# Attention scores by head and tile on quarters of the matrix array, in steps of half a pair of heads

## The chip, the cores and the metric

One core of a Trainium2 chip. Its engines are PE (matrix products and transposes; PEld is its weight load), DVE and ACT (vector and activation work; they alone read PSUM), POOL (GpSimd, SBUF only) and SP, whose queue issues nearly all DMAs. Each engine works through its own queue in order and waits on semaphores. The metric is the device time of one execution in microseconds, lower is better; a time is the median of several runs.

## The reference, cut to what matters

Local attention with block summaries (4 batches, 8 heads, 768 positions, 64 per head), then a soft mixture of experts over the 3,072 tokens of 512 numbers, then a routed mixture. The part around the change:

```python
k_sum = k.reshape(B, H, nb, block, D).max(axis=3)      # 24 blocks of 32
v_sum = v.reshape(B, H, nb, block, D).mean(axis=3)
scores_l = scale * q @ k.T, kept where |i - j| < 16    # scale = 1/8
scores_s = scale * q @ k_sum.T + log(block)
a = softmax(concat([scores_l, scores_s], axis=-1))
out = a @ concat([v, v_sum])
logits = x @ phi                                       # x: out as (3072, 512); phi: 32 slots
```

All of it is float32.

## The kernel before

The 32 heads are worked off as 16 pairs (the two heads of a pair lie on partitions 0 to 63 and 64 to 127 of q and k). The 768 queries of a pair are 12 tiles of 64; a tile sees a window of 96 keys and the 24 block maxima, 120 columns (KW). For each pair:

- t_sum (L294) takes maxima over blocks of k on DVE, puts the 24 of them into k's tile with three small maxima (L308), and copies them into six places (L309), so that one slice of k holds window and maxima of a tile.
- q_prep (L285) copies q on DVE and on ACT or POOL into a block-diagonal tile of 128 x 128 for each query tile; its off-diagonal blocks are zeros, written once by the memsets of L228.
- s_pe (L311): one product per query tile for both heads, 128 x 128 stationary against 120 columns, four tiles to a PSUM bank. A float32 product is two PE instructions, so that four tiles are eight. Rows 0 to 63 of the result belong to one head, the others to the other.
- s_max (L322), DVE: adds the mask, multiplies by -1/8 and takes the row minimum, in one instruction per tile. s_exp (L341), ACT: one exponential per tile, with the row's extremum as its bias.
- p_pe (L347): four transposes into a PSUM bank; p_ev (L355) copies them out on ACT. v_pe (L360): 8 products (16 instructions) with v, whose 65th column of ones gives the denominator. v_norm (L378): three DVE instructions that divide into X.
- vs_pe, vs_dist, vs_out, vs_in (L253 to L283): block means of v. 24 PE instructions (on four strips of 32 columns), an ACT copy, a second product that brings the means to their rows, a second ACT copy, and two POOL copies (L280) into v's tile.
- x_pe, x_ev, x_log: X transposed, copied by ACT, multiplied by phi into the logits lp. At the end of a batch (four pairs) moe_a to moe_d keep a running softmax over tokens: moe_a (L428) extremum, exponential and a copy; moe_b (L456) four transposes; moe_b_ev eviction into L; moe_c (L476) twelve products with X into pa.

The work goes in steps u of a third of a pair (four tiles), 48 of them and a tail. The schedule is manual: each engine gets its instructions in the order in which the loop from L614 writes them. A step first does what earlier steps have prepared: copies of step u-3, maxima and exponentials of u-1, normalising of u-4; then PE's products: scores of u, transposes of u-2, values of u-3:

```python
if inr(u - 3): p_ev(u - 3)
if inr(u - 1): s_max(u - 1); s_exp(u - 1)
...
if inr(u): s_pe(u)
if inr(u - 2): p_pe(u - 2)
...
if inr(u - 3): v_pe(u - 3)
```

moe_a, moe_b and moe_b_ev of a batch come at u = 20 and 21 + 12b, moe_c at 21 + 12b. PSUM has eight banks: three for transposes, copies and sums (tag tr), two for s, two for po, one for lp. On SP, load_qk and load_v fetch the pair three ahead (1.65 MB a pair), and load_w fetches the 32 tiles of 1 MB of expert weights at the steps listed in W_STEPS; the tiles take buffers as v's tiles, X and the four fix tiles come free. At U_END the running softmax is closed; then the expert products (ph at L756, pO at L832, from w) and the routed part follow.

## Time and profile before

| what | us |
|---|---|
| median of 3 runs (290.44 to 291.0) | 290.75 |
| the profiled execution | 292.63 |
| its span, first to last instruction | 290.9 |
| busy PE / DVE / ACT / POOL | 264.1 / 176.7 / 158.1 / 53.6 |
| L317, the score products, x384 | 57.5 |
| L344, the exponentials, x192 | 60.4 |
| L329, mask and maxima, x192 | 42.6 |
| mean granted PE clock | 0.954 |

A profile is of one execution, so sums are made against its 292.63 us. Rows of the timeline give start, duration, engine, line, operation, written and read tiles, shapes and a count; consecutive instructions of one kind are merged. A matmul's duration runs until its last result, so the start of the next group shows how long PE's queue was held. The granted clock is a share of 2.4 GHz: 1.00 is 2.4 GHz, 0.50 is 1.2 GHz. "idle before" is the time that the engine sat idle ahead of the instruction, with what ended it.

### The profile page before, as it was taken

How to read it: one execution, taken by the hardware profiler on the slowest of the kernel's cores; microseconds unless marked ns; L12 is line 12 of the kernel's file. 1: busy time of each engine (PE TensorE's matmuls, PEld its weight loads, DVE VectorE, ACT ScalarE, POOL GpSimd, SP SyncE). 2: the span in 40 equal slices, each digit the busy share in tenths (PEclk: the TensorE clock that was granted, in tenths of full speed). 3: DMA queues.
4: the chain of work that ended last, by engine and by line, in shares of the span. 5: the costliest groups of instructions: out<-in, count | busy, mean ns of one | idle time of the engine just before them, and what ended most of it. 6: DMA issues, size and time to landing. Idle time of an engine off the chain costs nothing.

```text
span 290.9 us, 7301 instructions
## 1 busy us (share of the span) xinstructions
PE 264.1 (91%) x2686; PEld 185.9 (64%) x2686; DVE 176.7 (61%) x798; ACT 158.1 (54%) x411; POOL 53.6 (18%) x78
## 2 busy tenths in 40 slices
PE   5899999997999979999969999999899999769990
PEld 1689888886688856888856844323256683546770
DVE  4499888985788885797854633116112547555950
ACT  2588876784568755568755731122323647923550
POOL 2122212230442123142302001000010361010000
PEclk9999999997999997999998999999999959996997
DMA  6999989899198997356455899999959100011893
GB/s 216 404 391 385 368 308 324 293 335 325 53 359 259 288 351 262 90 183 231 146 189 165 266 392 400 394 386 387 333 172 379 37 0 0 0 30 43 321 392 119
DMA packets 33657, 72.55 MB, mean 249 GB/s; under 512 B 2713, under 2 KB 4377, under 8 KB 33617
## 3 DMA queue, kind: packets, MB, share of 16 engines
q1 hardware_dynamic: 33552, 71.83, 69.3%
q8 instruction: 23, 0.38, 0.5%
q0 software_dynamic: 64, 0.20, 0.3%
q14 instruction: 18, 0.14, 0.1%
HBM read 65.73 MB, written 6.29 MB: 248 GB/s over the span
## 4 chain that ended last, share of the span: by engine, by line
PE 75%; DVE 14%; ACT 3%; issue 2%; DMA 2%; SPq 1%; DVEq 0%; ACTq 0%
PE s L317 15%; PE po L369 8%; PE pt L352 6%; PE pO L832 5%; PE ph L756 5%; PE pv L262 4%; PE pht L1049 4%; PE tx L402 3%; PE lp L420 3%; PE pa L491 3%; DMA vw<-in_vw_dram 2%; PE py L1292 2%; DVE fix L329 2%; PE py L1293 2%; PE py L1294 2%
## 5 line engine op out<-in xcount | busy, mean ns | idle before, releaser
L317 PE MATMUL s<-fix,fix 128*128 128x120 f32 x384 | 57.5, 295 | 0.3 <-DVE fix L291 0.3
L317 PEld LDWEIGHTS s<-fix,fix 128*128 128x128 f32 x384 | 48.6, 198 | 8.7 <-issue 6.3
L280 POOL COPY vw<-vw 24x780 f32<-24x780 f32 x32 | 26.8, 837 | 103.6 <-ACT vw L270 100.5
L344 ACT ACTIVATE fix<-fix,nb 128x120 f32<-128x120 f32 x128 | 40.3, 394 | 9.4 <-DVE nb L329 9.4
L329 DVE CUSTOM_DVE_ANT_0 fix<-s,con 128x120 f32<-128x120 f32 x128 | 28.5, 277 | 21.4 <-PE s L317 15.2
L369 PEld LDWEIGHTS po<-vw,pts 120*64 120x64 f32 x768 | 26.8, 139 | 11.1 <-issue 5.4
L369 PE MATMUL po<-vw,pts 120*64 120x65 f32 x768 | 33.5, 230 | 0.0
L357 ACT COPY pts<-pt 120x512 f32<-120x512 f32 x48 | 28.4, 593 | 7.9 <-PE pt L352 7.6
L270 ACT COPY vw<-pv 128x130 f32<-128x130 f32 x32 | 8.6, 270 | 30.7 <-PE pv L262 27.8
L386 DVE TENSOR_TENSOR X<-po,den 128x256 f32<-128x256 f32 x48 | 20.4, 424 | 1.7
L262 PE MATMUL pv<-vw,con 120*32 120x130 f32 x384 | 14.8, 278 | 6.9 <-DVE L L470 5.1
L352 PE MATMUL pt<-con,fix 128*120 128x128 f32 x128 | 20.7, 288 | 0.0
L344 ACT ACTIVATE sm<-sm,nb 128x120 f32<-128x120 f32 x64 | 20.1, 393 | 0.0
L1062 DVE CUSTOM_DVE_ANT_0 hlo<-pht,scr 128x1024 fp32r<-128x1024 f32 x11 | 13.3, 1213 | 10.0 <-PE pht L1049 10.0
L1049 PE MATMUL pht<-cT,gs 128*128 128x512 f32 x48 | 16.7, 476 | 0.6 <-ACT hhi L1073 0.4
L1073 ACT ACTIVATE hhi<-pht,scr 128x1024 fp32r<-128x1024 f32 x13 | 14.5, 1115 | 3.9 <-PE pht L1049 3.7
L832 PE MATMUL pO<-w,hx 128*32 128x512 f32 (+1 forms) x160 | 16.2, 514 | 0.0
L412 ACT COPY xT<-tx 128x512 f32<-128x512 f32 (+1 forms) x32 | 14.9, 464 | 2.1 <-PE tx L402 2.1
L402 PE MATMUL tx<-con,X 128*128 128x128 f32 x96 | 15.9, 274 | 0.0
L329 DVE DVE_READ_ACCUMULATOR2_ANT nb<- 128x1 f32 x192 | 15.8, 82 | 0.0
L262 PEld LDWEIGHTS pv<-vw,con 120*32 120x32 f32 x384 | 9.9, 109 | 9.1 <-DVE L L470 5.7
L352 PEld LDWEIGHTS pt<-con,fix 128*120 128x120 f32 x128 | 15.5, 147 | 0.1
(242 smaller groups left out, 426.2 us busy)
## 6 DMA issues: line engine op xcount, KB each, us to landing
w<-in_moe_w_dram SPq DMA_DIRECT2D x30, 1024.0 KB, 8.4
vw<-in_vw_dram SPq DMA_DIRECT2D x32, 390.0 KB, 8.6
fix<-in_kT_dram SPq DMA_DIRECT2D x15, 484.0 KB, 4.8
out_dram<-Y SPq DMA_DIRECT2D x24, 256.0 KB, 2.6
qn<-in_qT_dram SPq DMA_DIRECT2D x8, 384.0 KB, 5.1
fix<-in_qT_dram SPq DMA_DIRECT2D x7, 384.0 KB, 5.0
w1e<-in_moe_w_dram SPq DMA_DIRECT2D x4, 512.0 KB, 5.6
w2e<-in_moe_w_dram SPq DMA_DIRECT2D x4, 512.0 KB, 9.3
```

The lines of the kernel that those rows point to most:

```text
L262: nc.tensor.matmul(pv[32 * g : 32 * g + 32, 0:130], con[:KW, b0 : b0 + 32], vw[:KW, par, x0 : x0 + 130], start=c == 0, stop=c == 2,)
L280: nc.gpsimd.tensor_copy(st_["vw", n][row0 : row0 + NB, par].rearrange("p (s x) -> p s x", s=6), vo[row0 : row0 + NB, 130:260].unsqueeze(1) ...
L317: nc.tensor.matmul(sp[:, i, :], qbds[n % NQB][:, t, :], kTs[n % NKT][:, o : o + KW], start=True, stop=True)
L329: nc.vector.tensor_tensor_reduce(out=sm[:, i, :], in0=sp[:, i, :], in1=con[:, m0 : m0 + KW], scale=-0.125, scalar=3.0e38, op0=ALU.add, op1 ...
L344: nc.scalar.activation(sm[:, i, :], sm[:, i, :], AF.Exp, bias=nb_[:, i : i + 1], scale=-1.0)
L352: nc.tensor.transpose(pv[:, i, :], pr[:, i, :], ident)
L357: nc.scalar.copy(pts, st_.pop(("pt", u)))
L369: nc.tensor.matmul(po[64 * i : 64 * i + 64, c, j, :], pts[:, 2 * c + i, j * 64 : j * 64 + 64], vw[:KW, i, (t // 2) * 130 + 65 * j : (t // ...
L386: nc.vector.tensor_tensor(out=X[:, 2 * g : 2 * g + 2, 2 * hp * D : (2 * hp + 2) * D].rearrange("p c (j d) -> p c j d", j=2), in0=po[:, :, ...
L402: nc.tensor.transpose(pt[:, c * P : c * P + P], st_["X", b][:, c0 + c, hp * P : hp * P + P], ident)
L832: nc.tensor.matmul(po[c][32 * g : 32 * g + 32, 0 : cs.stop - cs.start], hTs[r][:, fc, 32 * g : 32 * g + 32], w[:, g, cs], start=(r, fc) in ...
L1049: nc.tensor.matmul(ph[:, c * 512 : c * 512 + 512], G[:, k * P : (k + 1) * P], cTt(1024 * j + 512 * c, 512), start=True, stop=True,)
```

## The change

Steps become halves of a pair (NU = 32, six query tiles each). s_pe makes a product for each head and tile, 64 x 64 stationary: its rows of the array are those of the head j, its columns those of the tile's parity i, so the four products of a pair of tiles lie on four quarters; head j has its own PSUM bank, and rows 0 to 63 of a result are an even tile, 64 to 127 an odd one. q is read as it was loaded; q_prep and the memsets go, and q gets three buffers. The masks shrink to three. s_exp subtracts the extremum on GpSimd, three tiles at once, and takes one exponential of 360 columns on ACT. t_sum writes the 24 maxima once and then takes the maxima of both halves straight into all six places. p_pe and its copy, v_pe and v_norm work on three tiles of two heads. The loop is written anew: scores, maxima and exponentials of u, then values and normalising of u-2, then the V-block sums, transposes of X, logits and batch ends, then transposes and copies of u-1. moe_a, moe_b and moe_c come at u = 13, 14 and 16 + 8b. s has three banks, po one. The weights are asked for at other steps. The order of the block means (C_DIST) is changed to fit.

The diff, cut to its core; removed lines of functions and of the loop are those of the kernel above and are mostly left out, as are shapes of PSUM tiles, masks and index constants:

```diff
-VS_FIRST = (0, 2)
-
 C_STEPS = (6, 7, 8, 9, 10, 11, 12, 13)
-W_X, W_BIG2, W_BIG3 = 14, (13, 15, 16, 17), (20, 21)
-U_END = 20 + 12 * (B - 1)
-W_STEPS = (*range(6, 36, 3), 39, 41, 43, 45, 46, 48, 49, 50, 51, 52)
+W_X, W_BIG2, W_BIG3 = 17, (13, 14, 16, 18), (20, 21)
+U_END = 13 + 8 * (B - 1)
+W_STEPS = (*range(4, 26, 2), 27, 29, 30, 30, 31, 32, 32, 33, 33)
...
-        ps_s = es.enter_context(tc.tile_pool(name="ps_s", bufs=2, space=PSUM))
-        ps_o = es.enter_context(tc.tile_pool(name="ps_o", bufs=2, space=PSUM))
+        ps_s = es.enter_context(tc.tile_pool(name="ps_s", bufs=3, space=PSUM))
+        ps_o = es.enter_context(tc.tile_pool(name="ps_o", bufs=1, space=PSUM))
...
+        NU = 2 * NPAIR
+        kTs = [fix[2][:, 0:KTW], fix[0][:, 0:KTW], fix[0][:, KTW : 2 * KTW]]
+        qns = [fix[2][:, KTW : KTW + S], fix[1][:, 0:S], fix[1][:, S : 2 * S]]
+        sms = [fix[3][:, i * 6 * KW : (i + 1) * 6 * KW].rearrange("p (j c x) -> p j c x", j=2, c=3) for i in range(2)]
+                nc.sync.dma_start(out=qns[0][:, 0:384], in_=qT[0, :, 0:384])
+            nc.sync.dma_start(out=kTs[n % 3], in_=kTd[n])
+            nc.sync.dma_start(out=qns[n % 3], in_=qT[n])
...
-        def q_prep(n):
...
+            hb = hm[:, 0:48].rearrange("p (b r) -> p r b", r=2)
+            nc.vector.tensor_tensor(out=kT[:, 32 : 32 + NB], in0=hb[:, 0], in1=hb[:, 1], op=ALU.max)
+            nc.vector.tensor_tensor(
+                out=kT[:, 32 + NB :].rearrange("p (c x) -> p c x", x=152)[:, :, 128:152],
+                in0=hb[:, 0:1].to_broadcast([P, 6, NB]),
+                in1=hb[:, 1:2].to_broadcast([P, 6, NB]),
+                op=ALU.max,
+            )
+
+        def s_pe(u):
+            n, h = divmod(u, 2)
+            sp = [ps_s.tile([P, 512], F32, tag="s", name=f"s{u}_{j}")[:, 0 : 3 * KW] for j in range(2)]
+            sp = [x.rearrange("p (c x) -> p c x", c=3) for x in sp]
             for c in range(3):
+                for i in range(2):
+                    t = 6 * h + 2 * c + i
+                    o = _koff(t)
+                    for j in range(2):
+                        nc.tensor.matmul(
+                            sp[j][64 * i : 64 * i + 64, c, :],
+                            qns[n % 3][64 * j : 64 * j + 64, 64 * t : 64 * t + 64],
+                            kTs[n % 3][64 * j : 64 * j + 64, o : o + KW],
+                            start=True, stop=True,
+                        )
             st_["s", u] = sp
 
+        def s_max(u, j):
+            sp = st_["s", u][j]
+            if j == 0:
+                st_["nb", u] = p3.tile([P, 2, 3], F32, tag="nb", name=f"nb{u}")
+            for c in range(3):
+                e = 3 * (u % 2) + c
+                m0 = C_MASK + (0 if e == 0 else 2 if e == 5 else 1) * KW
                 nc.vector.tensor_tensor_reduce(
+                    out=sms[u % 2][:, j, c, :],
+                    in0=sp[:, c, :],
                     in1=con[:, m0 : m0 + KW],
                     scale=-0.125,
                     scalar=3.0e38,
                     op0=ALU.add,
                     op1=ALU.min,
+                    accum_out=st_["nb", u][:, j, c : c + 1],
+                )
+
+        def s_exp(u, j):
+            sm = sms[u % 2][:, j]
+            nc.gpsimd.tensor_tensor(
+                out=sm, in0=sm, in1=st_["nb", u][:, j].unsqueeze(2).to_broadcast([P, 3, KW]), op=ALU.subtract
+            )
+            nc.scalar.activation(sm, sm, AF.Exp, scale=-1.0)
 
         def p_pe(u):
+            pts = p2.tile([KW, 2, 3, P], F32, tag="pts", name=f"pts{u}")
+            for j in range(2):
+                pt = ps_tr.tile([P, 512], F32, tag="tr", name=f"pt{u}_{j}")[:KW, 0 : 3 * P]
+                pt = pt.rearrange("p (c x) -> p c x", c=3)
+                for c in range(3):
+                    nc.tensor.transpose(pt[:, c, :], sms[u % 2][:, j, c, :], ident)
+                nc.scalar.copy(pts[:, j], pt)
             st_["pts", u] = pts
 
         def v_pe(u):
+            n, h = divmod(u, 2)
             pts = st_.pop(("pts", u))
             vw = st_["vw", n]
+            po = ps_o.tile([P, 3, 2, 65], F32, tag="po", name=f"po{u}")
+            for c in range(3):
                 for j in range(2):
                     for i in range(2):
+                        x0 = (3 * h + c) * 130 + 65 * j
                         nc.tensor.matmul(
                             po[64 * i : 64 * i + 64, c, j, :],
+                            pts[:, j, c, 64 * i : 64 * i + 64],
+                            vw[:KW, i, x0 : x0 + 65],
                             start=True,
                             stop=True,
                         )
             st_["po", u] = po
...
+            den = p3.tile([P, 3, 2], F32, tag="den", name=f"den{u}")
+                out=X[:, 3 * h : 3 * h + 3, 2 * hp * D : (2 * hp + 2) * D].rearrange(
+                in1=den.unsqueeze(3).to_broadcast([P, 3, 2, 64]),
+        XP = ((0, 3), (3, 3))
...
+        last = B - 1
+
+        def vs(n):
+            vs_pe(n)
+            vs_out(n, 0)
+
+        def vs2(n):
+            vs_dist(n)
+            vs_out(n, 1)
+            vs_in(n)
+
+        for u in range(NU + 11):
             inr = lambda w: 0 <= w < NU
+            m, odd = divmod(u, 2)
             if inr(u):
                 s_pe(u)
+                for j in range(2):
+                    s_max(u, j)
+                    s_exp(u, j)
             if inr(u - 2):
+                if (u - 2) % 8 == 0:
+                    st_["X", (u - 2) // 8] = xp.tile([P, 6, DM], F32, tag="X", name=f"X{(u - 2) // 8}")
+                v_pe(u - 2)
+                v_norm(u - 2)
+            if u == 1:
+                p_pe(0)
+                vs(0)
+                vs2(0)
+                vs(1)
+                vs2(1)
+            vn = m + 1 if odd and 0 < m < NPAIR - 1 else None
+            if vn is not None:
+                vs(vn)
+            if (n := at(u, 3, 2, NPAIR)) is not None:
+                x_pe(n, 0)
+                x_ev(n, 0)
+            if (n := at(u, 4, 2, NPAIR)) is not None:
+                x_pe(n, 1)
+                x_ev(n, 1)
+            if (n := at(u, 6, 2, NPAIR)) is not None:
                 x_log(n)
+            if (b := at(u, 13, 8, B)) is not None:
+                moe_a(b)
+            if (b := at(u, 14, 8, B - 1)) is not None:
+                moe_b(b)
+                moe_b_ev(b)
+            if (b := at(u, 16, 8, B - 1)) is not None:
+                moe_c(b)
+                moe_c_ev(b)
+            for i in range(3):
+                if (b := at(u, 16 + i, 8, B)) is not None:
+                    moe_d(b, i)
+            if vn is not None:
+                vs2(vn)
+            if inr(u - 1) and u > 1:
+                p_pe(u - 1)
+            if odd and m + 1 < NPAIR:
+                t_sum(m + 1)
             if u == U_END:
                 keep_warm(2)
                 si_max()
@@ -661,7 +660,7 @@
                 moe_b(last)
                 moe_c(last, 0)
                 keep_warm(1)
+                moe_b_ev(last)
                 si_bc()
                 si_bc_ev()
                 moe_c(last, 1)
@@ -672,25 +671,16 @@
                 keep_warm(1)
                 siT_done()
                 keep_warm(1)
             if u == 0:
                 load_qk(2)
                 load_v(2)
+            if odd and m < NPAIR - 3:
+                load_qk(m + 3)
+                load_v(m + 3)
             if u == 3:
                 nc.sync.dma_start(out=con[:, C_SEL:], in_=consts[:, C_SEL:])
                 nc.sync.dma_start(out=phis, in_=phi.rearrange("(c p) s -> p c s", p=P))
+            for _ in range(W_STEPS.count(u)):
                 load_w()
     big3.append(ctx.enter_context(tc.tile_pool(name="big3", bufs=len(W_BIG3))))
```

## Rows read from the trace of the kernel before

**Rows 1.** Windows: stretch, span, busy PE, PEld, DVE, ACT, POOL; clock, DMA, GB/s
```profile
39.52:48.17 8.65, 8.65 (x125) 7.37 (x122) 7.16 (x42) 6.21 (x19) 2.86 (x3) 1.00 0.92 322
...
56.83:68.24 11.41, 9.51 (x130) 7.78 (x126) 9.12 (x48) 6.78 (x21) 2.85 (x3) 1.00 0.91 318
68.24:80.33 12.09, 12.09 (x135) 9.25 (x135) 7.82 (x39) 6.52 (x20) 3.35 (x4) 0.86 0.48 160
```

**Rows 2.** Timeline of PE: start, duration, instruction, count, idle before
```profile
68.24 0.88 PE L262 MATMUL pv<-vw,con 120*32 120x130 f32 x24 [1.63 <-DVE L L470]
...
72.99 1.92 PE L491 MATMUL pa<-X,L 128*32 128x512 f32 x12
...
80.33 0.88 PE L262 MATMUL pv<-vw,con 120*32 120x130 f32 x24
81.13 1.15 PE L317 MATMUL s<-fix,fix 128*128 128x120 f32 x8
82.12 0.61 PE L352 MATMUL pt<-con,fix 128*120 128x128 f32 x4
82.56 0.39 PE L273 MATMUL pv<-vw,con 128*128 128x130 f32 x2
82.88 0.69 PE L369 MATMUL po<-vw,pts 120*64 120x65 f32 x16
83.50 1.15 PE L317 MATMUL s<-fix,fix 128*128 128x120 f32 x8
...
85.46 0.63 PE L420 MATMUL lp<-xT,phis 128*32 128x256 f32 x6
```

**Rows 3.** Lines by form, POOL: count, busy us, mean ns, idle before
```profile
L518 POOL TENSOR_TENSOR ce_all<-L,mx 128x192 f32<-128x192 f32 x4 | 2.0, 507 | 17.3 <-DVE mx L517 17.3
...
L928 POOL TENSOR_TENSOR Y<-Y 128x384 f32<-128x384 f32 x1 | 1.0, 1002 | 0.1
...
L1119 POOL TENSOR_TENSOR scr<-scr 128x256 f32<-128x256 f32 x1 | 0.6, 616 | 2.3 <-ACT scr L1118 2.3
```

**Rows 4.** Lines by form, ACT
```profile
L522 ACT ACTIVATE ce_all<-ce_all 128x192 f32<-128x192 f32 x4 | 1.5, 365 | 2.0 <-POOL ce_all L518 2.0
...
L933 ACT ACTIVATE scr<-scr 128x24 f32<-128x24 f32 x1 | 0.2, 211 | 0.0
```

**Rows 5.** Timeline of all engines, at the start and about 158
```profile
7.79 1.21 PE L317 MATMUL s<-fix,fix 128*128 128x120 f32 x8
...
9.04 0.28 DVE L329 CUSTOM_DVE_ANT_0 fix<-s,con 128x120 f32<-128x120 f32 x1 [0.23 <-PE s L317]
...
9.86 0.08 DVE L329 DVE_READ_ACCUMULATOR2_ANT nb<- 128x1 f32 x1
...
157.89 0.34 DVE L517 TENSOR_REDUCE mx<-L 128x6 f32<-128x192 f32 x1
...
158.38 0.51 POOL L518 TENSOR_TENSOR ce_all<-L,mx 128x192 f32<-128x192 f32 x1 [1.63 <-DVE mx L517]
```

**Rows 6.** Timeline of all engines, in mid-batch
```profile
42.84 1.74 POOL L280 COPY vw<-vw 24x780 f32<-24x780 f32 x2 [6.92 <-ACT vw L270]
...
43.50 0.37 DVE L308 TENSOR_TENSOR fix<-hm 128x8 f32<-128x8 f32 x3
...
43.90 0.78 DVE L309 COPY fix<-fix 128x144 f32<-128x144 f32 x1
```

**Rows 7.** Timeline of PE at three places, and one window of DMA
```profile
15.78 1.12 PE L317 MATMUL s<-fix,fix 128*128 128x120 f32 x8 [0.25 <-DVE fix L291]
...
151.31 2.06 PE L317 MATMUL s<-fix,fix 128*128 128x120 f32 x8
...
168.48 1.15 PE L420 MATMUL lp<-xT,phis 128*32 128x256 f32 x6
...
216.77 1.07 PE L832 MATMUL pO<-w,hx 128*32 128x256 f32 x16
...
210.00:215.00 5.00, 4.59 (x65) 2.58 (x69) 0.93 (x6) 2.02 (x4) 1.01 (x6) 1.00 0.23 63
```

More of the change, by code (lines that the diff above doesn't have):

```diff
@@ L78, in _constants @@
         m[:, ssl] = 8.0 * LOGB
-        c[:64, C_MASK + var * KW : C_MASK + (var + 1) * KW] = m
-        c[64:, C_MASK + var * KW : C_MASK + (var + 1) * KW] = m
+        for e in range(3):
+            if var == (2 if e == 0 else 0) or var == (3 if e == 2 else 1):
+                r0 = 64 * (var % 2)
+                c[r0 : r0 + 64, C_MASK + e * KW : C_MASK + (e + 1) * KW] = m
     for g in range(4):
@@ L279, in vs_in @@
             for row0, par in ((32, 0), (96, 1)):
-                nc.gpsimd.tensor_copy(
+                eng = nc.vector if n == 0 and par else nc.gpsimd
+                eng.tensor_copy(
                     st_["vw", n][row0 : row0 + NB, par].rearrange("p (s x) -> p s x", s=6),
@@ L304, in t_sum @@
             )
-            hb = hm[:, 0:48].rearrange("p (h c q b r) -> p r c b q h", h=2, c=3, q=2, b=2)
-            ks = kT[:, 32:56].rearrange("p (q h c b) -> p c b q h", q=2, h=2, c=3)
-            for c in range(3):
-                nc.vector.tensor_tensor(out=ks[:, c], in0=hb[:, 0, c], in1=hb[:, 1, c], op=ALU.max)
-            nc.vector.tensor_copy(kTv[:, :, 128:152], kT[:, 32:56].unsqueeze(1).to_broadcast([P, 6, 24]))
-        def s_pe(u):
-            n, g = divmod(u, 3)
-            sp = ps_s.tile([P, 4, KW], F32, tag="s", name=f"s{u}")
-            for i in range(4):
-                t = 4 * g + i
-                o = _koff(t)
-                nc.tensor.matmul(
-                    sp[:, i, :], qbds[n % NQB][:, t, :], kTs[n % NKT][:, o : o + KW], start=True, stop=True
-                )
-            st_["s", u] = sp
@@ L322, in s_max @@
-        def s_max(u):
-            g = u % 3
-            sp = st_.pop(("s", u))
-            sm = sms[u % 3].rearrange("p (i x) -> p i x", i=4)
-            nb_ = p3.tile([P, 4], F32, tag="nb", name=f"nb{u}")
-            for i in range(4):
-                m0 = C_MASK + _var(4 * g + i) * KW
+            hb = hm[:, 0:48].rearrange("p (b r) -> p r b", r=2)
[6 more added lines that the diff above has]
+            )
@@ L611, in tile_kernel @@
         t_sum(0)
-        q_prep(0)
-        for u in range(NU + 32):
-            inr = lambda w: 0 <= w < NU
-            if inr(u - 3):
-                p_ev(u - 3)
-            if inr(u - 1):
-                s_max(u - 1)
-                s_exp(u - 1)
-            if (n := at(u, 1, 3, NPAIR - 1)) is not None and n or u == 2:
-                t_sum(n + 1 if n else 1)
-                q_prep(n + 1 if n else 1)
-            if inr(u - 4):
-                if (u - 4) % 12 == 0:
-                    st_["X", (u - 4) // 12] = xp.tile([P, 6, DM], F32, tag="X", name=f"X{(u - 4) // 12}")
-                v_norm(u - 4)
-            for i in range(2):
-                if (n := at(u, 8 + i, 3, NPAIR)) is not None:
-                    x_ev(n, i)
-            for r, f in enumerate((moe_a, moe_b_ev, moe_c_ev)):
-                if (bb := at(u, 20 + r, 12, B)) is not None and (r < 2 or bb < B - 1):
-                    f(bb)
-            for i in range(3):
-                if (bb := at(u, 22 + i, 12, B)) is not None:
-                    moe_d(bb, i)
+        last = B - 1
@@ L639, in tile_kernel @@
+        def vs(n):
[6 more added lines that the diff above has]
+        for u in range(NU + 11):
+            inr = lambda w: 0 <= w < NU
+            m, odd = divmod(u, 2)
             if inr(u):
                 s_pe(u)
+                for j in range(2):
+                    s_max(u, j)
+                    s_exp(u, j)
             if inr(u - 2):
-                p_pe(u - 2)
-            for n in range(NPAIR):
-                if u == (VS_FIRST[n] if n < 2 else 3 * n - 1) + 1:
-                    vs_dist(n)
-                    vs_out(n, 1)
-                    vs_in(n)
@@ L648, in tile_kernel @@
-            for i in range(2):
-                if (n := at(u, 7 + i, 3, NPAIR)) is not None:
-                    x_pe(n, i)
-            if (n := at(u, 10, 3, NPAIR)) is not None:
-                x_log(n)
-            if inr(u - 3):
-                v_pe(u - 3)
-            last = B - 1
+                if (u - 2) % 8 == 0:
[8 more added lines that the diff above has]
+                vs2(1)
@@ L674, in tile_kernel @@
                 keep_warm(1)
-            for r, f in enumerate((moe_b, moe_c)):
-                if (bb := at(u, 20 + r, 12, B)) is not None and bb < last:
-                    f(bb)
-            for n in range(NPAIR):
-                if u == (VS_FIRST[n] if n < 2 else 3 * n - 1):
-                    vs_pe(n)
-                    vs_out(n, 0)
             if u == 0:
@@ L684, in tile_kernel @@
                 load_v(2)
-            if (n := at(u, 2, 3, NPAIR - 3)) is not None:
-                load_qk(n + 3)
-            if (n := at(u, 1, 3, NPAIR - 3)) is not None:
-                load_v(n + 3)
+            if odd and m < NPAIR - 3:
+                load_qk(m + 3)
+                load_v(m + 3)
             if u == 3:
```

73 lines of the change are left out of this document (10 added, 63 removed).

## The prediction

> **What bounds the kernel now.** I read the windows pair by pair first. A pair of heads in mid-batch takes 8.65 us and PE is busy for all of it; DVE has 1.5 us to spare, ACT 2.4, and the DMA rings run at 0.92 [rows 1]. So until the logits are done the end is set by PE, and its timeline gives the prices: eight score instructions hold the queue 0.99 us (81.13 to 82.12), four transposes 0.44, the second V-block product 0.32, sixteen value instructions 0.62, the 24 V-block sums 0.80, six logit instructions about 0.56 [rows 2]. Three score groups make 3 us of the 8.65.
>
> The second reading is the batch ends. The two pairs around the first take 11.41 and 12.09 us [rows 1], 6.2 more than two plain ones; two more batch ends look alike. Only 2.3 of it is work (pa 1.9, four transposes 0.44). In the first of these pairs PE is idle for 1.9 us, its longest wait being 1.63 us on DVE's eviction of L; in the next its granted clock averages 0.86, that is, part of it ran at 1.2 GHz [rows 1, 2]. This loss comes from moe_a, moe_b and the eviction following one another within one step.
>
> After the logits (168.48 and about 1.1 us more [rows 7]) come some 121 us of expert work that the diff leaves alone.
>
> **The change, part by part.** I call one u of the new loop a step: two to a pair, odd ones carry the V-block work.
>
> *Scores.* 384 instructions on the whole array become 768 on quarters, 24 a step. What a quarter costs isn't in the trace. Nearest are the V-block sums: four strips at once, 130 columns, 0.80/24 = 33 ns each [rows 2]. Floor: a pa instruction of 512 columns on three strips costs 1.92/12 = 160 ns, scaled to 120 columns and four tiles 28. Ceiling: today's 0.99/8 = 124 ns with only two of four tiles at once, 62. I take 35, near the sums: 0.84 us a step, 1.7 a pair where 3.0 stand now. All else on PE keeps its count (48 value instructions, 12 transposes to a pair), so PE's work falls to about 7.4 us a pair. Were PE still the bound, that would be 1.3 us times 16.
>
> *But the loop is no longer staggered.* Before, step u evicted, maximised and exponentiated what earlier steps had left. After it, ACT's queue holds, in this order: exp(u,0), exp(u,1), the V-block copy, x_ev, the second V-block copy, the copies of p_pe(u-1). Both exponentials need this step's own scores, by way of DVE and GpSimd, and everything behind them waits too. From the start of an odd step:
> - scores 0.84; DVE starts 0.2 after the last issue (group at 7.79, DVE at 9.04, 1.25 where the queue is held 1.0) [rows 5]
> - first three maxima: four took 9.04 to 9.94, so three 0.70 [rows 5]
> - hand-over to GpSimd 0.15 (158.23 to 158.38) [rows 5]
> - two subtractions of 360 columns. Broadcast rows give 507 ns at 192 and 616 at 256, so 790 at 360; two full operands took 1002 at 384, about 950 at 360, my upper bound [rows 3]. 2 x 0.79 = 1.58; DVE's second trio lies beside it.
> - ACT: 211 ns at 24 columns, 365 at 192, so 520 at 360 [rows 4]; its start after GpSimd I estimate at 0.05, at most the 0.15 above.
>
> That is 4.05 us. Then the V-block copy (about 0.2 behind the exponential), vs_dist on PE 0.32, six transposes 0.66: the next step starts at 5.25. PE's own work in an odd step is only 4.0, so it idles 1.25. The even step has nothing on PE that waits for its own exponential: scores 0.84, values 0.92, three transposes 0.42, logits 0.56, six transposes 0.7, together 3.45. A pair is 8.7 against 8.65: **the time won on the array goes into the wait.** What is late next is the value products of the odd step (their copies come 1.75 after its start); they end with the V-block sums and transposes at 3.9, before 4.3, and cost nothing. Bounds: scores at 28 ns take 0.2 off each step; subtractions at 0.95 add 0.3 to the odd one.
>
> *Off the path.* ACT gets 4 exponentials of 0.52 a pair for 12 short ones; q_prep goes from DVE, ACT and GpSimd; normalising is done in two calls. All had slack, cost nothing and gain nothing. GpSimd takes 4 x 0.79 beside two copies of 0.87 [rows 6]: 4.9 of 8.7. The s banks (three, two to a step) are freed by DVE within the step; the one value bank is freed a step before its next use.
>
> *Block maxima.* Two tensor_tensor with two SBUF inputs replace three small ones and a copy. They come 5.0 us into the odd step, when GpSimd starts its two V copies, and the next maxima need DVE at 6.25. Rows: while L280 ran from 42.84 to 44.58, three L308 took 0.37 and were not held, but the copy L309 took 0.78 and ended as GpSimd did [rows 6]. I charge nothing here, at most one copy's 0.65, which fits before 6.25. The Trainium skill, SBUF — State Buffer, "Who interferes with whom", says a DVE instruction with two SBUF inputs is fully blocked for the whole GpSimd instruction. L308 disagrees, L309 agrees. By that rule the sum would be the rival of the port below.
>
> *Batch ends.* moe_a, moe_b and moe_c now lie in steps 13, 14 and 16, each with a step between to be evicted in. I leave the 2.3 of work and 0.75 for moe_a's DVE and ACT work ahead of the V-block copy: 3.05 where 6.2 stands now, -3.15 three times, **-9.5**.
>
> *Start.* Step 1 holds both first V-block sums, with t_sum(1) behind a DVE copy that waits for them. By the prices above p_pe(0) ends near 13, the two V chains near 16.7, t_sum(1) near 18.3, when pair 1's scores start; now 15.78 [rows 7]. **+2.5.**
>
> *End.* Now 168.48 plus 1.1 less 151.31 [rows 7] is 18.3 from the last pair's first scores, 14.9 without the batch end's 3.4. After: 3.45 for step 30, then one after the other: exponential 4.05, copies 1.2, values 0.9, transposes and logits 1.0, pa 1.9, transposes 0.7, copies 0.8, values 0.9, normalising 1.0, last transposes, copy and logits 1.6 (durations as above, copies and normalising estimated at 0.45 and 0.95 each): 17.5 in all, less pa 15.6. **+0.7.**
>
> *DMA.* A pair still moves 1.65 MB and about one weight tile, 2.7 MB in 8.7 us, as now. On SP load_qk, load_v and load_w keep their order; each pair waits for the release of its k buffer. Weights 13 to 19 are asked for in steps 30 to 33, as early against the logits as now. The rings are idle from 210 to 215 (0.23 busy) while pO's last tiles run on to 217.8 (216.77 and 1.07) [rows 7], which covers the few us by which consumption moves up. Nothing.
>
> Sum: 14 pairs x 0.05 = +0.7, +2.5, +0.7, -9.5 = **-5.6 us**. The profiled execution took 292.6 (span 290.9); the sum gives it 287.0, and the median of 290.75 becomes **285.2**.
>
> **Rivals.**
> - *PE or a shorter chain decides* (faster still): if ACT's copy can start by 3.5 rather than 4.05 and scores cost 28 ns, a pair is 7.8, -0.9 x 14 beyond the sum, 273. For: every hand-over is one row only. Against: the chain has 4 us of durations from rows. 15%.
> - *The port* (slower): both tensor_tensor wait for both V copies, DVE is free at 7.0, the next maxima come 0.8 late, so do the copies for the values, and from an extra 0.35 on the odd step stretches with them: +0.5 x 14 = +7, 292. It decides if L309's behaviour is the rule and L308's the exception [rows 6]. 18%.
> - *The clock.* Every odd step idles 1.25 us. At the batch end 1.9 us of idle in 11.4 was followed by a stretch at 1.2 GHz worth 1.5 us (12.09 less 8.65 less pa) [rows 1, 2]. If this comes in every pair, +1.0 to 1.5 x 14, 299 to 306. Against: the gaps are in pieces of at most 0.9. 13%. The Trainium skill, TensorE: Matmul & The Clock Gate, Part 1, second failure mode, warns of frequent small idles that make the clock oscillate; rows 1 and 2 show a fall only after the long one.
> - *Quarters don't run side by side* (the change doesn't do what it says): 62 ns an instruction, +0.65 a step, +1.3 x 15 = +19, 304. Against: strips do run side by side. 8%.
> - The forecast itself: 46%.
>
> **How the numbers follow.** The forecast's own range is 279 to 290 (subtractions at the bound +4, scores at the floor -5). The whole range must leave out no more than 2 in 10: the far half of the first rival and the upper parts of the clock and the quarters go, so 274 to 300. Below 0.2% (0.6 us) a measurement of this kernel can't tell a difference from none. Faster: the first case, nearly all of the forecast and a little of the port, 0.61; same 0.05; slower 0.34 from the port, the clock and the quarters.
>
> **What would show it.** Right: pair windows of 8.7 with PE idle about 1.2; the V-block copy on ACT starting 4 to 4.3 us after the odd step's first score, its wait put down to the exponential and that to GpSimd; 24 score instructions in 0.8; no pair over 11 us and no clock of 0.86 at batch ends. Wrong: score groups over 1.2 us; tensor_tensor of t_sum at 0.8 or more; granted clock under 0.95 over the attention; pair windows under 8.0, which would mean that ACT does not queue as the loop is written.

## The result and the profile after

The changed kernel takes **293.48 us** (median of five, 292.42 to 294.52) against 290.75 for the kernel before (five beside it, 288.82 to 291.0): a ratio of 1.0104, 95% interval 1.0061 to 1.0147. A later set on another occasion gave 293.17 against 289.44, ratio 1.0122 (1.005 to 1.0194). It is slower by about 1%, where 2% faster was forecast. In all runs below the medians are of all executions, while the ratios leave out those over 1.5% above the fastest of their version. The profiled execution of after took 292.89 us with a span of 291.1; that of before took 292.63 and was 1.9 above the median of its kernel, so the two profiles differ by less than the medians do.

Where the time went is read from the first scores of pairs. The timeline of PE, before (start, duration, instruction, count):

```profile
23.19 1.15 PE L317 MATMUL s<-fix,fix 128*128 128x120 f32 x8
...
57.64 1.15 PE L317 MATMUL s<-fix,fix 128*128 128x120 f32 x8
...
89.79 1.15 PE L317 MATMUL s<-fix,fix 128*128 128x120 f32 x8
...
139.59 0.59 PE L317 MATMUL s<-fix,fix 128*128 128x120 f32 x3
```

and after, with idle time ahead of an instruction and what ended it in brackets:

```profile
26.70 0.85 PE L302 MATMUL s<-fix,fix 64*64 64x120 f32 x24
...
60.89 0.85 PE L302 MATMUL s<-fix 64*64 64x120 f32 x24
61.66 0.92 PE L354 MATMUL po<-vw,pts 120*64 120x65 f32 x24
...
64.36 0.85 PE L302 MATMUL s<-fix 64*64 64x120 f32 x24
65.61 1.18 PE L354 MATMUL po<-vw,pts 120*64 120x65 f32 x24 [0.41 <-ACT pts L342]
...
68.42 0.49 PE L260 MATMUL pv<-vw,con 128*128 128x130 f32 x2 [0.35 <-ACT vw L257]
68.75 0.82 PE L341 MATMUL pt<-con,fix 128*120 128x128 f32 x6
71.29 1.05 PE L302 MATMUL s<-fix,fix 64*64 64x120 f32 x24 [1.72 <-DVE fix L285]
...
75.81 0.54 PE L341 MATMUL pt<-con,fix 128*120 128x128 f32 x3 [0.77 <-ACT xT L397]
...
91.75 0.85 PE L302 MATMUL s<-fix 64*64 64x120 f32 x24
...
140.01 0.84 PE L302 MATMUL s<-fix,fix 64*64 64x120 f32 x24
...
150.60 1.68 PE L302 MATMUL s<-fix 64*64 64x120 f32 x24 [1.90 <-DVE fix L285]
...
160.93 1.69 PE L354 MATMUL po<-vw,pts 120*64 120x65 f32 x24 [1.87 <-ACT pts L342]
...
171.29 1.13 PE L584 MATMUL warm<-con 128*128 128x256 f32 x4
...
179.86 0.64 PE L746 MATMUL ph<-w,siT 128*32 128x512 f32 x4
```

After less before, pair by pair: pair 2 starts 3.5 us later (26.70 against 23.19), pair 6 3.3 (60.89, 57.64), pair 9, behind the first batch end, 2.0 (91.75, 89.79), pair 14, behind the second, 0.4 (140.01, 139.59). Pair 15 starts 0.7 earlier (150.60; before in [rows 7]). Then it is lost again: the logits are done at 171.29 where the warm-up products behind them stood at 169.56, and the first product of the experts is at 179.86 instead of 178.21, 1.65 later. So the start cost 3.5, the plain pairs behind it gave 0.3, two batch ends with the plain pairs around them gave 1.3 and 1.5, the third with its pair 1.1, and the last pair cost 2.4.

The windows of after show a step each: an even and an odd step in mid-batch, the pair they make, then steps 13, 14 and 16 of the first batch end (step 15 is a plain odd one of 5.13), and five stretches for the clock. Columns are the stretch, its length, busy us (instructions) of PE, PEld, DVE, ACT and POOL, granted clock, DMA share and GB/s.

```profile
43.67:47.14 3.47, 3.47 (x65) 2.49 (x64) 2.13 (x15) 1.25 (x4) 3.04 (x4) 1.00 0.89 323
47.14:52.28 5.14, 4.34 (x85) 3.29 (x84) 3.56 (x19) 3.57 (x10) 1.70 (x3) 1.00 1.01 341
43.67:52.28 8.61, 7.81 (x148) 5.79 (x147) 5.69 (x34) 4.82 (x13) 4.74 (x7) 1.00 0.96 334
...
64.36:71.29 6.93, 4.41 (x85) 3.30 (x84) 4.56 (x21) 4.57 (x13) 3.20 (x4) 1.00 0.93 307
71.29:76.29 5.00, 4.23 (x68) 2.98 (x68) 2.85 (x17) 1.76 (x4) 1.53 (x2) 1.00 0.65 248
...
81.42:86.61 5.19, 5.19 (x77) 2.99 (x76) 2.81 (x17) 2.24 (x6) 3.04 (x4) 1.00 0.87 321
...
10.00:20.00 10.00, 6.67 (x109) 4.64 (x102) 4.78 (x26) 3.74 (x10) 5.23 (x7) 0.88 1.03 403
...
110.00:120.00 10.00, 7.20 (x142) 5.29 (x143) 6.73 (x36) 3.45 (x9) 3.91 (x5) 1.00 0.65 230
...
150.00:160.00 10.00, 8.46 (x124) 6.62 (x124) 5.67 (x33) 3.21 (x8) 3.58 (x5) 0.83 0.73 240
```

The pair is 8.61 us against 8.65 [rows 1], but PE is busy for 7.81 of it, no longer for all: PE has stopped being the bound. A batch end's four steps take 22.25 us; four plain ones would take 17.22 (twice 8.61). That is 5.0 more, where 6.2 stood before and 3.05 was forecast.

What is late in the odd step, and what more is late at a batch end, stands in the timelines of ACT, GpSimd and DVE of step 13 in after, with one row each of GpSimd and DVE from the odd step before it (60.73 and 60.37):

```profile
66.96 0.51 ACT L333 ACTIVATE fix<-fix 128x360 f32<-128x360 f32 x1 [1.02 <-POOL fix L330]
67.71 0.50 ACT L333 ACTIVATE fix<-fix 128x360 f32<-128x360 f32 x1 [0.24 <-POOL fix L330]
68.12 0.25 ACT L257 COPY vw<-pv 128x130 f32<-128x130 f32 x1
...
68.64 0.48 ACT L421 ACTIVATE LT<-lp,nm_run 96x256 f32<-96x256 f32 x1
...
60.73 1.72 POOL L268 COPY vw<-vw 24x780 f32<-24x780 f32 x2 [1.66 <-issue]
...
66.14 1.54 POOL L330 TENSOR_TENSOR fix<-fix,nb 128x360 f32<-128x360 f32 x2 [1.86 <-DVE nb L317]
69.48 1.72 POOL L268 COPY vw<-vw 24x780 f32<-24x780 f32 x2 [1.80 <-issue]
...
60.37 0.18 DVE L285 TENSOR_TENSOR fix<-hm 128x24 f32<-128x24 f32 x1
...
69.24 0.42 DVE L422 COPY LT<-lp 96x256 f32<-96x256 f32 x1 [1.09 <-ACT LT L421]
69.58 0.15 DVE L277 TENSOR_REDUCE hm<-fix 128x1 f32<-128x16 f32 x1
...
70.63 0.60 DVE L285 TENSOR_TENSOR fix<-hm 128x24 f32<-128x24 f32 x1
```

GpSimd's subtraction and ACT's exponential, which the prediction sized from [rows 3, 4], by line:

```profile
L330 POOL TENSOR_TENSOR fix<-fix,nb 128x360 f32<-128x360 f32 x64 | 49.2, 789 | 48.0 <-DVE nb L317 48.0
...
L333 ACT ACTIVATE fix<-fix 128x360 f32<-128x360 f32 x64 | 32.3, 504 | 74.9 <-POOL fix L330 74.9
```

**The chain of the odd step** is as the prediction drew it. From the first score at 64.36 the subtraction starts after 1.78 us, the exponential after 2.60, and the V-block copy (L257) after 3.76, behind both exponentials on ACT's queue.

**The batch end** has a wait that the prediction does not contain. On DVE moe_a stands ahead of t_sum. Its copy L422 waits 1.09 us for moe_a's exponential L421 on ACT, which itself waits its turn there behind x_ev. Only then does DVE begin the block maxima of the next pair, at 69.58. By then GpSimd copies V sums (from 69.48), and L285 takes 0.60 instead of the 0.18 of the pair before, where t_sum came ahead of GpSimd's copies. PE, with its transposes issued, stands for 1.72 us until the next pair's keys are complete.

### The profile page after: what moved, and what is told of

The parts are those of the page before. It is cut to its first block, busy times and chain, and to the rows that moved or that the text cites. A ratio compares the mean times of both kernels' runs of the same rounds, so it can differ in the third digit from the quotient of the medians.

```text
span 291.1 us, 7899 instructions
## 1 busy us (share of the span) xinstructions
PE 245.6 (84%) x3070; PEld 158.4 (54%) x3070; DVE 153.7 (53%) x699; ACT 127.7 (44%) x289; POOL 91.5 (31%) x131
## 4 chain that ended last, share of the span: by engine, by line
PE 37%; DVE 5%; ACT 4%; DMA 3%; issue 2%; POOL 2%; SPq 1%; DVEq 0%; ACTq 0%; POOLq 0%
PE ph L746 5%; PE pO L822 4%; PE pht L1039 3%; DMA w2e<-in_moe_w_dram 3%; PE py L1282 2%; PE py L1284 2%; PE py L1283 2%; PE po L354 2%; DVE hlo L1052 2%; POOL fix L330 2%; PE s L302 1%; PE pa L476 1%; PE warm L584 1%; PE pc L194 1%; PE tx L387 1%
## 5 line engine op out<-in xcount | busy, mean ns | idle before, releaser
L333 ACT ACTIVATE fix<-fix 128x360 f32<-128x360 f32 x64 | 32.3, 504 | 74.9 <-POOL fix L330 74.9
L330 POOL TENSOR_TENSOR fix<-fix,nb 128x360 f32<-128x360 f32 x64 | 49.2, 789 | 48.0 <-DVE nb L317 48.0
L317 DVE CUSTOM_DVE_ANT_0 fix<-s,con 128x120 f32<-128x120 f32 x192 | 41.7, 279 | 40.5 <-PE s L302 39.3
L342 ACT COPY pts<-pt 120x384 f32<-120x384 f32 x64 | 27.8, 483 | 6.2 <-PE pt L341 5.0
L302 PE MATMUL s<-fix,fix 64*64 64x120 f32 x480 | 18.4, 277 | 4.6 <-DVE fix L285 4.2
L371 DVE TENSOR_TENSOR X<-po,den 128x384 f32<-128x384 f32 x32 | 17.8, 558 | 1.1
L302 PEld LDWEIGHTS s<-fix,fix 64*64 64x64 f32 x480 | 13.4, 136 | 8.5 <-DVE fix L285 4.8
L397 ACT COPY xT<-tx 128x384 f32<-128x384 f32 x32 | 15.1, 472 | 4.3 <-PE tx L387 4.3
L1039 PE MATMUL pht<-cT,gs 128*128 128x512 f32 x48 | 15.9, 454 | 0.7 <-ACT hhi L1063 0.5
L317 DVE DVE_READ_ACCUMULATOR2_ANT nb<- 128x1 f32 x192 | 15.9, 83 | 0.0
L278 DVE TENSOR_REDUCE hm<-fix 128x48 f32<-128x768 f32 x16 | 15.1, 944 | 0.5 <-DMA fix<-in_kT_dram 0.5
L746 PE MATMUL ph<-w,siT 128*32 128x512 f32 x128 | 14.8, 596 | 0.1
```

Source lines behind the costliest of these rows:

```text
L302: nc.tensor.matmul(sp[j][64 * i : 64 * i + 64, c, :], qns[n % 3][64 * j : 64 * j + 64, 64 * t : 64 * t + 64], kTs[n % 3][64 * j : 64 * j + ...
L317: nc.vector.tensor_tensor_reduce(out=sms[u % 2][:, j, c, :], in0=sp[:, c, :], in1=con[:, m0 : m0 + KW], scale=-0.125, scalar=3.0e38, op0=A ...
L330: nc.gpsimd.tensor_tensor(out=sm, in0=sm, in1=st_["nb", u][:, j].unsqueeze(2).to_broadcast([P, 3, KW]), op=ALU.subtract)
L333: nc.scalar.activation(sm, sm, AF.Exp, scale=-1.0)
L342: nc.scalar.copy(pts[:, j], pt)
L746: nc.tensor.matmul(ph[32 * g : 32 * g + 32, :], siT[:, kc, :], w[:, g, :], start=kc == 0, stop=kc == 3)
```

## Experiments

Three theories stood at the outset. A: ACT's queue order sets the odd step, and DVE's the batch end. B: the DMA rings set the pace. C: PE with its short gaps is still the bound, and the chain beside it is not. Where a run needed another, its expectation names it.

**moe_a behind t_sum.** In the loop's program, one call moves:

```diff
-            if (b := at(u, 13, 8, B)) is not None:
-                moe_a(b)
...
             if odd and m + 1 < NPAIR:
                 t_sum(m + 1)
+            if (b := at(u, 13, 8, B)) is not None:
+                moe_a(b)
```

> Of the kernel after, moe_a's instructions alone are moved behind t_sum in the step. Theory A (the block maxima queue on DVE behind moe_a's copy, which waits for ACT): the three idle stretches of PE ahead of the next pair's scores (1.72, 1.90 and 1.90 us) go, and with the third the slower groups behind it (about 1 us): 5.5 to 6.5 us less, 287 to 288 us. Theory B (DMA sets the pace, so that time won in one step is lost in the next): under 1 us, 292.5 to 293.5.

288.77 us, ratio to before 0.9966 (0.9932 to 1.0). That is 4.7 below the 293.48 of after (4.0 by the two ratios), somewhat less than expected and far from theory B. The windows of step 14 and of all four steps of the first batch end:

```profile
69.50:74.82 5.32, 4.02 (x68) 2.81 (x67) 2.95 (x18) 2.90 (x8) 3.04 (x4) 1.00 0.88 324
...
64.35:85.14 20.79, 17.60 (x309) 12.31 (x308) 13.08 (x73) 11.16 (x29) 9.48 (x12) 1.00 0.83 295
```

Step 13 is a plain odd step again (5.15, from 64.35 to 69.50), and the four take 3.57 more than plain ones. Step 14 stays 1.85 over a plain even step. Its extra work is moe_b's four transposes into pn (0.4 us). Since pn takes one of the three tr banks, the second half of p_pe waits until x_ev, which stands behind the exponentials on ACT, has read another: 1.30 us here, 0.77 in after, 1.55 at the third batch end of this version.

**The exponentials at the end of the step.**

```diff
         def s_exp(u, j):
             nc.gpsimd.tensor_tensor(
...
-            nc.scalar.activation(sm, sm, AF.Exp, scale=-1.0)
+        def a_exp(u):
+            for j in range(2):
+                sm = sms[u % 2][:, j]
+                nc.scalar.activation(sm, sm, AF.Exp, scale=-1.0)
...
                 p_pe(u - 1)
+            if inr(u) and u > 1:
+                a_exp(u)
```

(in steps 0 and 1 they stay where they were)

> Of the kernel after, only the place of the two exponentials in a step's program is moved: behind the V-block copies, x_ev and p_pe's copies instead of ahead of them. Theory A (the place on ACT's queue sets the odd step): odd steps fall from 5.14 to between 4.0 and 4.3 us, the even ones stay at 3.45, a pair takes 7.5 to 7.8; with 14 pairs 11 to 15 us less, 278 to 282 us. Theory B (DMA): rings at about 0.93 of 8.6 us let a pair fall to 8.0 and no further while weights are loaded: 5 to 7 us less, 286 to 288. Theory C (PE with its short gaps is the bound): pairs stay at 8.6 and the time at 293.

283.31 us, ratio 0.9751 (0.9694 to 0.9809): 10 below after, a little short of the 11 to 15 that theory A promised, and the pair is not what A said. It takes 8.39, with the odd step at 4.72 instead of 5.14:

```profile
37.91:42.63 4.72, 4.09 (x84) 3.19 (x84) 3.61 (x19) 3.35 (x10) 2.40 (x4) 1.00 0.95 318
42.63:46.30 3.67, 3.67 (x63) 2.67 (x63) 2.30 (x16) 1.37 (x4) 2.40 (x3) 1.00 0.97 354
```

What took over stands in PE's timeline of the same version, and in its groups by line (out<-in, count, then busy us, mean ns of one and idle us ahead):

```profile
42.63 1.05 PE L302 MATMUL s<-fix,fix 64*64 64x120 f32 x24 [0.63 <-DVE fix L285]
```

```profile
L285 DVE TENSOR_TENSOR fix<-hm 128x24 f32<-128x24 f32 x16 | 7.9, 497 | 0.5
```

With the chain gone, every pair's first scores wait for t_sum, which stands behind the normalisation on DVE and now meets GpSimd's V copies, since these come earlier: L285 takes 497 ns in the mean against 269 in after. A second chain, 0.4 us shorter by the odd step's length, had been hidden by the first. Half of what this version won is not in the pairs: its logits end 8.8 us earlier than in after, and 4.5 of that lies behind the first score of step 30, where after's profile had lost 2.0 to the clock (see the run of the end alone).

**Both edits.**

> The edits of the first two together. Theory A: their gains add up, 17 to 21 us less than the kernel after, 273 to 277 us, and faster than the kernel before too. Theory B (DMA): no more than 9 us less, 285.

274.68 us, ratio 0.9501 (0.9416 to 0.9586), as theory A said. The sum is more than the parts (18.8 below after against 4.7 and 10.2), in part because the batch-end waits had grown to 2.1 to 2.5 us in the version with the exponentials alone. Up to the first product of the experts the three profiles lie 15.9, 5.5 and 8.8 below after; the rest is the expert stretch behind, which no edit touches and which was 2.3 us shorter in this profile than in after's. The pair is still 8.4, with the same 0.63 of waiting. Its timelines show DVE and GpSimd meeting, the prediction's rival of the port:

```profile
41.72 0.49 DVE L285 TENSOR_TENSOR fix<-hm 128x24 f32<-128x24 f32 x1
42.14 0.30 DVE L286 TENSOR_TENSOR fix<-hm 128x144 f32<-128x144 f32 x1
...
41.35 1.79 POOL L268 COPY vw<-vw 24x780 f32<-24x780 f32 x2 [0.42 <-POOL fix L330]
```

L285 ends at 42.21, with the first of the two copies (that copy, taken by itself, took 0.83 and ended at 42.18), and L286 then runs at its 0.30 undisturbed.

**t_sum first on DVE, with both edits.**

```diff
                     s_exp(u, j)
+            if odd and m + 1 < NPAIR:
+                t_sum(m + 1)
             if inr(u - 2):
...
-            if odd and m + 1 < NPAIR:
-                t_sum(m + 1)
```

> The version with both edits, and t_sum put directly behind the step's maxima, ahead of the normalisation, on DVE. In that version the odd step's end is set by a wait of 0.63 us for the block maxima, of which 0.3 is the tensor_tensor standing still while GpSimd copies V sums (0.49 instead of 0.18). Theory A (DVE's order sets what is left): the wait goes in 13 odd steps, odd steps 4.1 us, pairs 7.5 to 7.7, 8 us less, 266 to 268 us. Theory B (DMA rings at 0.90 to 0.97 in these stretches cap the pair at about 8.1): 4 us less, 271.

266.65 us, ratio 0.9226 (0.9139 to 0.9313), as theory A said. A pair in an early stretch (a later one, 82.61 to 90.10, is as long):

```profile
33.89:41.38 7.49, 7.49 (x148) 5.68 (x147) 5.60 (x34) 4.72 (x13) 4.74 (x6) 1.00 1.04 395
```

PE is busy throughout: 7.49 us is PE's work, against the 7.4 that the prediction had reckoned for it. The DMA rings are full there at 395 GB/s and do not stretch the pair, so theory B falls; two other pairs of this version, between 45 and 61 us, take 7.6 and 7.95, and how much of that is the DMA's was not tried.

**t_sum first, alone.** The same move in the kernel after.

> The kernel after with t_sum directly behind the step's maxima as its one edit. Theory A (in mid-batch the exponential's place on ACT sets the step, the block maxima have time to spare and matter at batch ends alone): pairs stay at 8.6, the three batch-end waits go, 287 to 289 us, the same as with moe_a moved. Theory D (the block maxima hold every odd step): pairs fall to 8.0, 279 to 281 us.

287.32 us, ratio 0.9868 (0.9827 to 0.9909), as theory A said. By ratio it lies 1% under the version with moe_a moved, more than the intervals leave to chance; the two profiles, at mean clocks of 0.953 and 0.954, took 289.38 and 288.79, so at the same clock the two moves come out nearly alike. Pairs stay at 8.61 (first scores at 43.65 and 52.26), the batch-end wait is gone. So in mid-batch neither of the two orders is worth much alone: the exponentials' place gives 0.2 a pair, t_sum's gives nothing, both together 1.1.

**Without GpSimd's subtraction.**

```diff
-            nc.gpsimd.tensor_tensor(
-                out=sm, in0=sm, in1=st_["nb", u][:, j].unsqueeze(2).to_broadcast([P, 3, KW]), op=ALU.subtract
-            )
-            nc.scalar.activation(sm, sm, AF.Exp, scale=-1.0)
+            for c in range(3):
+                nc.scalar.activation(sm[:, c], sm[:, c], AF.Exp, bias=st_["nb", u][:, j, c : c + 1], scale=-1.0)
```

> Of the kernel after, the subtraction on GpSimd is left out and the maximum goes into the exponential as a bias, six exponentials of 120 columns a step instead of two of 360. Theory A (the chain from DVE over GpSimd to ACT sets the odd step): two subtractions of 0.77 and one hand-over leave the chain, 0.8 of ACT comes in, so the V-block copy starts 0.5 to 0.7 us earlier, pairs take 7.9 to 8.1, 7 to 10 us less, 284 to 287 us. Theory C (the chain is not the bound): ACT gets 1.6 us more work a pair and nothing else changes: 293, or some us more.

The time, 286.6 us, is in theory A's range, but its four executions run from 281.15, below that range, to 287.76, so that the time alone decides nothing and no ratio is given. Pairs come in two lengths, 8.73 (43.19 to 51.92) and 7.98 (94.59 to 102.57). The timelines of GpSimd and DVE in one of each:

```profile
51.70 1.74 POOL L268 COPY vw<-vw 24x780 f32<-24x780 f32 x2 [6.99 <-ACT vw L257]
...
98.76 1.89 POOL L268 COPY vw<-vw 24x780 f32<-24x780 f32 x2 [3.10 <-issue]
...
51.77 0.94 DVE L286 TENSOR_TENSOR fix<-hm 128x144 f32<-128x144 f32 x1
...
98.76 0.30 DVE L286 TENSOR_TENSOR fix<-hm 128x144 f32<-128x144 f32 x1
```

Where GpSimd's first copy started 0.07 us ahead of L286, DVE stood until about the end of that copy, and most of the next pair's first scores with it. Where both start together, DVE takes its 0.30 and GpSimd's two copies take 1.89 instead of 1.74. The pair without the collision takes the 7.9 to 8.1 that theory A said.

**Without the subtraction, t_sum first.**

> The version without the subtraction on GpSimd, and t_sum directly behind the step's maxima. In that version pairs of 8.73 us, in which the second tensor_tensor of t_sum takes 0.94 beside GpSimd's V copies, stand beside pairs of 7.98 in which it takes 0.30. Theory E (these collisions on the port cost 0.75 a pair): without them all plain pairs take 7.9 to 8.0 and the batch-end waits go too: 274 to 277 us. Theory A without the port: only the batch-end waits go, 280 to 282 us.

272.11 us, ratio 0.9366 (0.93 to 0.9431): theory E, and a little better than it said. All plain pairs looked at take 7.9, and L286 has a mean of 302 ns against 621. So 0.64 us on one instruction (0.94 to 0.30) cost 0.75 on the pair (8.73 to 7.98) once t_sum was on the path.

**The subtraction twice.** The softmax does not feel the second shift.

> The kernel after with GpSimd's subtraction issued twice (a second shift by the maximum, which the normalisation takes out again). Theory A (the subtractions are on the chain that sets the odd step): odd steps grow by 1.4 to 1.6 us, even ones stay at 3.47, pairs take 10.0 to 10.2, 20 to 24 us more, 313 to 317 us. Theory C (they lie beside other work): GpSimd is busy 8.1 of 8.6 us a pair and the time grows by under 3 us.

333.4 us (two executions). The direction is theory A's, the size is neither's. Where the clock is at 1.00 a plain pair takes 10.34, close to the 10.0 to 10.2 expected:

```profile
55.92:66.26 10.34, 7.82 (x148) 5.79 (x147) 5.69 (x34) 4.71 (x13) 7.81 (x11) 1.00 0.69 246
```

That makes 24 us of the 40. The rest was not taken apart: PE's longest wait is past 2 us in most of the odd steps looked at, and the granted clock falls in many places: 0.67 from 20 to 30 us, 0.66 from 110 to 120, 0.911 over the whole span against 0.958 in after. The rival of the clock in the prediction exists, then, but in plain pairs only this version, with its longer chain, shows it.

**The end alone.** The exponentials at the end of the step from step 29 on, and the kernel after unchanged beside it.

> The kernel after with the exponentials moved behind the step's copies on ACT from step 29 on alone, so that mid-batch is as it was. Theory A (at the end the value products of step 30 wait 1.87 us for copies that stand behind step 31's exponentials, and PE runs slower behind that wait): from step 30's first score to the last logits 16 to 17.5 us instead of 20.7, 3 to 4.5 us less, 289 to 290.5 us. Theory F (the end is lost to the clock that fell behind the batch-end wait at 150 us): at most 1.5 us less.

> The kernel after, unchanged, beside the others on the same chip: 292.4 to 294.5 us.

288.3 us, ratio 0.9965 (0.9918 to 1.0012), against 293.17 and 1.0122. The wait of 1.87 is gone (0.52 stands there), and from step 30's first score to the last logits it takes 17.67 us. But this run does not settle the size: the unchanged kernel took 20.69 there in its first profile and 18.69 in this second one. The windows of after, second execution, say why:

```profile
10.00:20.00 10.00, 7.68 (x125) 5.65 (x117) 4.58 (x30) 3.73 (x10) 5.78 (x8) 0.75 1.03 403
...
110.00:120.00 10.00, 8.95 (x139) 6.97 (x139) 5.17 (x30) 2.23 (x5) 2.89 (x5) 0.66 0.48 169
150.00:160.00 10.00, 7.33 (x129) 5.59 (x127) 6.62 (x36) 3.46 (x12) 4.02 (x6) 1.00 0.82 297
```

Here the clock fell behind the second batch end and held behind the third; in the first execution it was the other way round, with the same wait of 1.90 ahead of step 30's scores in both. At full clock the end is 18.69 us in after and 16.18 in the version with all exponentials late (146.27 to 162.45): 2.5 us of order. Part of the 4.9 us by which this run lies below after is at the start, where both programs are alike and the clock differs (below).

**The start.** On top of the version with both edits and t_sum first:

```diff
+                if u == 1:
+                    vs(0)
                 a_exp(u)
             if u == 1:
                 p_pe(0)
-                vs(0)
                 vs2(0)
-                vs(1)
-                vs2(1)
-            vn = m + 1 if odd and 0 < m < NPAIR - 1 else None
+            vn = 1 if u == 2 else m + 1 if odd and 0 < m < NPAIR - 1 else None
```

> The version before it, and at the start the first V-block chain ahead of the transposes, the second one moved from step 1 to step 2. Theory A (the start is order, not DMA): the scores of the second pair start near 13 instead of 17.6 us, 3 to 4 us less than the version before it. Theory B (the start waits for the DMA of the second pair's k and V): under 1 us less.

265.31 us, ratio 0.9157 (0.9088 to 0.9225): 1.3 less than the version before it, a difference inside the two intervals, and 8% faster than the kernel before with the same arithmetic as after. The scores of pair 1 do start at 13.35 instead of 17.15, but the next step's at 19.06 instead of 19.58: the value products of step 2 wait 1.52 us for GpSimd's copy of V sums. Neither theory; the gain ran into the next wait.

## Why the prediction was wrong

*What bounds the kernel, scores, the odd step: right.* 24 score instructions hold the queue 0.77 us (60.89 to 61.66), forecast 0.84; quarters do run side by side. A subtraction takes 0.79, an exponential 0.50, the V-block copy starts after 3.76 us, before the 4 to 4.3 of the forecast, and vs_dist on PE after 4.06 (68.42), forecast 4.25. The pair came to 8.61 against 8.7. The time won on the array went into the wait, and the runs that move the exponentials show that the wait is the queue's. What the text did not see is that a second chain, through t_sum on DVE, was only 0.4 us shorter, so that removing the wait alone is worth little in a pair; for the forecast of plain pairs that didn't matter.

*Block maxima: the charge of nothing held in plain pairs and failed at the batch ends.* L285 and L286 take 0.18 and 0.30 in mid-batch. The prediction took the three L308 and the copy L309 [rows 6] for two rows that disagree. They do not, and the trace of before had the rows that show it. Where GpSimd's copies began at 72.48, the three L308 took twice as long as in the prediction's window:

```profile
72.74 0.76 DVE L308 TENSOR_TENSOR fix<-hm 128x8 f32<-128x8 f32 x3
```

Another 0.54 stands at 84.20. Each time the first of the three ends with GpSimd's first copy, 0.83 us behind that copy's start; in the prediction's window this was nearly over when L308 came. The runs show one rule, that of issue order: a tensor_tensor on DVE that comes second waits for the end of the GpSimd instruction that is running, 0.18 to 0.49 or 0.60 for L285, 0.30 to 0.94 for L286. Where DVE comes first GpSimd loses less: 1.74 to 1.89, half of L286's 0.30. The Trainium skill, SBUF — State Buffer, "Who interferes with whom", also lets issue order decide which one blocks, a condition that the prediction left out, and DVE's waits agree with it; what they add is that of two GpSimd copies in a row only the running one is waited for.

*Batch ends: the step that failed.* It left 2.3 us of work and 0.75 for moe_a ahead of the V-block copy, 3.05 in all, and took that for the whole. The V-block copy that vs_dist waits for was not delayed at all: it stands ahead of moe_a's exponential on ACT. What was behind moe_a was t_sum on DVE, a queue that the step did not list, and behind t_sum the next pair's scores: 1.79 in step 13. Another 1.1 comes in step 14, beyond the 0.44 of moe_b's transposes, and 0.77 of it is the wait for a bank of PSUM. So 5.0 stands where 3.05 was put, and with the moe_a copy out of the way 3.57. Of the forecast gain of 3.15 each, the first two gave 1.3 and 1.5, with the plain pairs around them.

*End: the third batch end and the last pair together* were to give 3.15 less 0.7; they cost 1.3 from pair 14's first score on (pair 14 starts 0.4 late, the logits end 1.7 late). The steps from 31 on were sized well: from step 31's first score to the logits 13.7 at full clock (second execution of after) against 17.5 less 3.45. Step 30 was not: 5.0 instead of 3.45, for moe_b's transposes (0.44, counted in the batch end) and the bank, and step 29 holds the wait of 1.90. In the profiled execution another 2.0 went to the clock.

*Start: forecast +2.5 at the first scores of pair 1; measured +1.0 there and +3.5 at pair 2, and only part of it is order.* Pair 1's first scores start at 16.81 against 15.78, and all but four of them at 17.68, since L286 stood 0.96 us beside a copy of GpSimd (16.67 to 17.63). In the execution of the end-alone version, whose program is that of after up to step 28, the clock stayed at 1.00 from 10 to 30 us and pair 2 started at 24.39: +1.2, or +1.7 counted from each program's own first scores (7.31 there, 7.79 before). In both profiles of after the clock was 0.75 to 0.95 there, and pair 2 started at 26.70 and 26.86. The forecast counted too much order and no clock.

*DMA: nothing, right.* From the first product of the experts to the end of the span after takes 111.2 us and before 112.7; the versions above, which are alike there, take 109.0 to 112.7.

*The sum.* Forecast +0.7 in mid-batch, +2.5, -9.5 and +0.7, that is -5.6. Measured up to the experts: -0.3 in the plain pairs up to pair 6, +3.5, -2.8 from pair 6 to pair 14 with two batch ends, +1.3 from pair 14 to the last logits and -0.1 behind them, +1.65 in all. Against the forecast's parts the end with the third batch end misses by 3.8, the first two batch ends by 3.5, the start (at pair 2) by 1.0, and the plain pairs give 1.0 back: 7.2 together. The two whole profiles lie only 0.3 apart, for the expert stretch took 1.5 more in that of before, where nothing was changed; the medians are 2.7 apart, and no profile shows where before's other executions were shorter.

*Rivals.* The port is real, and was priced near the time that came out (292), but not for its reason: in mid-batch it costs nothing, since t_sum is done (60.47 and 0.30 for L286) as GpSimd's copies begin (60.73), which wait for the second V-block copy on ACT. It costs 0.4 to 0.5 us of each batch-end wait (L285 at 0.60 to 0.65 instead of 0.18) and, in the first profile, holds L286 0.66 longer at the start. The clock fell at the start and at batch ends, not in plain pairs. The shorter chain and the slow quarters did not come.

## What to carry to other kernels

When work leaves the engine that is the bound, write down for each other engine the whole order of its queue within a step, and for every instruction with a wait what stands behind it, through to the engine that was the bound. Moving moe_a behind t_sum changed no work and gave 4.7 us; placing the exponentials behind the copies, which do not need them, gave 10. Where two chains are nearly as long, an edit of either looks nearly worthless in the pairs, and only both together show what the change had won: 8.61 and 8.39 us a pair against 7.49.

## What was not expected of the hardware

The granted clock fell in different places in two executions of the same program with the same waits: 1.00 and 0.83 from 110 and 150 us in the one, 0.66 and 1.00 in the other, each behind an idle stretch of PE of 1.90 us. The same holds at the start (0.88 and 0.75, and 1.00 in a version alike up to there). So a wait of this length costs at times its own length alone, and at times some 2 us more. Nor does a longer wait always bring the fall: in the version with the exponentials late the clock was 1.00 behind two waits of 2.49 us (from 110 and from 150 us) and 0.85 behind one of 2.12 (from 70), and with moe_a moved it was 0.83 behind a wait of 1.55 (from 150). The Trainium skill, TensorE: Matmul & The Clock Gate, Part 1, tells of a kernel whose frequent short gaps make the clock swing; in the plain pairs of after, with 0.8 us of gaps in each, it stayed at 1.00.

The lock between DVE and GpSimd turns on small shifts: 0.07 us of lead decided in the version without the subtraction whether a pair took 8.73 or 7.98 us.
